# New written-out orders for kernel generation, two attention cores and two convolutions

## The chip, the cores and the metric

The kernel runs on one core of a Trainium2 chip. A core has five engines that run side by side, each from a queue of its own and each in the order of that queue: TensorE (PE in the profile; its weight loads are listed as PEld), VectorE (DVE), ScalarE (ACT), GpSimd (POOL) and SyncE (SP), which here issues DMA transfers. The metric is the device time of one execution in microseconds; lower is better. Times of several executions are given as their median.

## What is computed

The input x has 2048 rows of 512 values. Four layers follow one another, each adding its result to x: an attention, a long convolution, and both again with the same weights.

```python
x = x + _A_ref(_layernorm(x), A_wqkv, A_wo)
x = x + _B_ref(_layernorm(x), B_A_re, ..., B_Dskip)
x = x + _A_ref(_layernorm(x), A_wqkv, A_wo)
x = x + _B_ref(_layernorm(x), B_A_re, ..., B_Dskip)
```

The attention has 32 heads of 16 values. Each position looks at 8 positions: itself and those 2, 4, ... 14 before it. Logits, a softmax over the 8, a weighted sum of v, and a product with wo.

The convolution first makes, for each of the 512 channels, a kernel of 2048 values from a state of 128 complex numbers, then convolves each channel with it by Fourier transforms of length 4096, and adds u times Dskip:

```python
P = jnp.exp(logdA[:, :, None] * l[None, None, :])
K = jnp.einsum("dn,dnl,dn->dl", Cc, P, dB).real
...
y = irfft2(Uf * Kf)[..., :L] + u * Dskip
```

## The kernel before

**Stages.** The kernel goes through kernel generation together with the front of the first attention (0 to about 108 us), the first attention core (to about 191), the first convolution (to about 247), whose end overlaps the front of the second attention (about 243 to 273), the second core (to about 361) and the second convolution (to the end).

**What sets the order.** Inside each stage the instructions are emitted under `manual_schedule`: nothing reorders them, and each engine runs its queue as written. The order of a stage is a string. A function goes through its tokens and calls for each the small function that it stands for; that function puts its matmuls on PE's queue, its eviction on ACT's or DVE's, its transfers on SP's. So a string fixes the order of every queue at once. In the convolutions a token ends with the engine that evicts: `KD` is a step K evicted by DVE, `KA` by ACT.

**Kernel generation** (`ORDERK`, run by `k_gen`). The letters stand for the steps that build powers of the state (DVE products at L1115, ACT exponentials and sines), for the front of attention 1, and for the sums over the state on PE (L1273), whose results ACT evicts (L1281) and SP stores to `kd_dram` in 24 transfers (L1295). The front normalises the blocks `x_blk` (statistics, `ln_nb` at L1185, then an apply on DVE, L197, or ACT, L195; the table `ENGK` says which), transposes them on PE (L1201) and projects them (L1211).

**Attention core** (`CORE0`, `CORE1`, run by `LayerA.core`). The letters: `v` a projection of v (PE L398, ACT L400), `q` one of q (PE L223, ACT L225), `m` a product of q with the shifted k (DVE L342, 2.3 us), `l` its sum over the head (PE L350 or L354), `P` a product of the attention weights with the shifted v (DVE L472), `S` and `V` its sum (PE L487, L497), `O` the projection with wo (PE L508) with the statistics of the next norm, `a` to `f` and others steps of that norm. In `CORE0`, `1` and `6` load the two halves of the kernel from `kd_dram`, and `A` to `H` are its eight permuting copies `k_perm` (L1455), whose engines stand in `KROWS`. `w` loads `w_sb`, 4 MB of weights of the second transform stage (L596), into the place of q's and k's weights and of k, so it waits until the last product `m` has read them.

**Convolution** (`ORDER0` with the tail in `ORDERF`, then `ORDER1`, run by `FftB.run`). `K` and `U` are the first transform stage of the kernel and of the input (PE L807, eviction L796), `k` and `u` the second (PE L814; `k` evicted at L796, `u` always by ACT at L865), `m` the product of both spectra (DVE L852), `y` the first inverse stage (32 half matmuls, PE L883) and `Y` the same with 16 whole ones (PE L879), evicted at L796, `w` and `v` the second inverse stage, 8 or 4 blocks of rows for one group of columns (PE L927 to L929). `w` and `v` evicted by DVE add x on DVE (L931); evicted by ACT, x is added on PE by a further matmul and ACT copies (L933). In the first convolution every kernel spectrum is stored to `kf_dram` after its product and its buffer is used again by a later `k`; the second convolution loads them from there.

**Front of attention 2** (`ORDERF`, among the rest of the first convolution). `h`/`H`, `a`, `p` are statistics, `n` is the apply of a block (`D` DVE, `G` GpSimd and DVE in turns), `T` its transposes (PE L271), `E` a copy of half of them (L273), `P` and `Q` projections of k and q, `x` and `e` the copies that extend k.

Of the kernel before, what the change touches and what calls it, by code (L numbers as in the profile page):

```python
# [21 lines left out]
S = 2048  # L22
# [21 lines left out]
DQT = 8  # L44
NQT = DQG // DQT
ORDERK = """
isbCCisCbCiaisbMCiiMiMGGMsGCbicbMibMcsaTGMbiMsbicbTisTbGTMTTTiiGTaGbsaTibbciTGMTsibaMiMacGGTaalw
GMbMiaaMlWMMMalTsiyaMMyyyiMTMttaaMMdekaealTkMMbaMskMMalMKMaMqqkKiqMMWbQlMqqMHyyyUyaUUpQtxepakxkK
pqtUdUkpeUHUUQUkaUKUEqqUUkTQkU3TxTaqpqlKT3T3xalkQkKpkWTTxxTqlyq3kyyQppyqTKHTTxqQlWTUtktUekekklKx
KzkzkkkUUKUETUTzkkzttUUUUeKppUUUeKkkUEkxKkpoUkxpUxKXkUUKkxpUqxoUXpqxoQkppxKZXZxZ  # L50
"""
ORDER0 = """
KD KA KA KD KA KA KD KA KD KA KD kA KD KA KA KD UA UD UA kD kA UA kD UA UD UA
UA KD kD kA kD u m u u u kD UA m UA UA m u kD u m UD m kA UA kD UA
u m m UA UA kD kA u kD m u kA kA m u yD YD m u m u yA m u YA m
u u u m m m YA YA yA yD w000D YA yA
"""
LATE0 = "a s t g r b m"
ORDERF = """
yD yA yA yD yD YA w010A v101A v111A v110A h00 v100A h01 h11 w001A h10 a0 v112A S a1 p0 p1 n0D w011A  # L60
v102D T0 E01D n1G E00A v113D H2 v103A P02 a2 Q00 P01 p2 T1 E10D E11D P00 P03 n2G P11 P10 H3 P12 a3
T2 E20D p3 E21D n3D P13 P22 P23 T3 P20 E31D P21 E30D x1
"""
ORDER1 = """
UD UA UD UA UA UD UA UD UA UD UA u UD m u u u m u m UA u UA m m UA
UD u m m u u m u u yA m m yA yD m u u m u u YD m YA YA u w000A
yA yA m m m w001D yA yA w010D yA yA yA yA YD w011D YA v101D v102D v112D v111D v100A v110D v113A v103D
"""

CORE0 = """  # L70
vvvmvvlmqvqlxmevvlrmvlvnmlvmmTvqxllvqvvmqPemvqSrllPmqxn1OT0meVPrlP5S3POSqmOl2SPOSPOm4PlSlb7xn6O8
VOePSOdrAPSPPDnOSOSPCO9SbPOwHfPGVOfbPdFSBOEftSataaOfa
"""
CORE1 = """
0m1l2ml3mqqqlqmvvlmvvvmxqlemvvllrmvmnqlTqqmxvlmlevvvvqPvvvlmrPqlSnmmxOqSPTqeSPOPSlPOOmlSPrbSmnOP
SOwPllxdSOOVefPaaPaSrOnVPbOSOPSdPOPbVaOSdfOPatfaSfataO
"""
ROWS0 = (0, 2, 1, 3, 4, 5, 6, 7, 8, 9, 10, 11, 12, 13, 14, 15)
ROWS1 = (0, 2, 1, 3, 4, 5, 6, 7, 8, 9, 10, 11, 12, 13, 14, 15)
NCOL = (2, 2)  # L80
ENGK = dict(b="AAAAAAAAAAAAAAAAA", y="DAAAAAAAADAA", z="DAAA", e="AAAAAAAA", K="AAAAAAAAAAAAAAAA", Q="AAAAAAAA", x="AAAAAAAAAAAAAAAA")
STATD = (3,)
KROWS = "DADDDDDD"
VROWS = (*range(0, 16, 2), *range(1, 16, 2))


# [908 lines left out]
def k_gen(tc, nc, a_consts, ins, kd, la, x_v, lnst, zero, b_consts):  # L995
# [3 lines left out]
    with ExitStack() as ctx:  # L999
# [161 lines left out]
        def norms():  # L1161
            D2 = D * D
            for b in range(4):
                cs = slice(4 * b, 4 * b + 4)
                rstd = la.fp.tile([P, 4], F32, name="ln_rstd")
                nb = la.fp.tile([P, 4], F32, name="ln_nb")
                ln[b] = rstd, nb
                if b not in STATD:
                    mean, ms = lnst["s1"][:, cs], -1.0 / D
                    msq = la.fp.tile([P, 4], F32, name="ln_msq")  # L1170
                    veps = la.fp.tile([P, 4], F32, name="ln_veps")
                    lvar[b] = veps[:]
# [12 lines left out]
                yield lambda: nc.vector.scalar_tensor_tensor(nb[:], mean, ms, rstd[:], ALU.mult, ALU.mult)  # L1185
# [28 lines left out]
        def projected(kind, b, ft):  # L1214
            dst = la.kT[:, ft, 14 + b * 4:18 + b * 4, :] if kind == "k" else la.qT[b][:, ft]
            copy_by(ENGK["K" if kind == "k" else "Q"][4 * b + ft])(dst.rearrange("p a q -> p (a q)"), pps[kind, b, ft][:])  # L1216

# [59 lines left out]
        def produced(c, q8):  # L1277
            if (c, q8) == (0, 0):
                late["kgs"] = late["kgp"].tile([P, NB * 4, P], BF16, name="kgs")
            q0 = c * CH + q8 * 8  # L1280
            copy_by(ENGK["x"][c * CH // 8 + q8])(late["kgs"][:, :, q0:q0 + 8].rearrange("p m (h j) -> p m h j", h=2),  # L1281
                           pks[c, q8][:, :, 0:4 * NB * 4].rearrange("p h (j m) -> p m h j", j=4))
# [38 lines left out]
        def calls(f, *args):  # L1321
            return [lambda a=a: f(*a) for a in args]

        def chain(*fs):
# [59 lines left out]
def kernel(  # L1384
# [68 lines left out]
    def k_part(h, j):  # L1453
        cp = nc.scalar.copy if KROWS[h * 4 + j] == "A" else nc.vector.tensor_copy
        cp(kp[:, h * 64 + j * 16:h * 64 + (j + 1) * 16, :, :],  # L1455
           krs[h][:, :, j * 64:(j + 1) * 64].rearrange("p a (q r) -> p q a r", r=4))
# [128 lines left out]
```

## Time and profile before

| | us |
|---|---|
| median of three executions | 406.82 (406.75, 406.82, 409.1) |
| the profiled execution | 408.58 |
| its span, first to last instruction | 406.80 |

The profile is of one execution. "Busy" is the time in which an engine runs an instruction that does work. A row of a group has the busy time, the mean of one instruction, and after the second bar how long the engine stood idle just ahead of them and on whom it waited. A row of the timeline has the start, the duration, the engine, line and operation, and in brackets the idle time before it and what released it. `x4` in such a row means four like instructions in one row; their durations overlap a little at the ends, so the step from start to start is shorter than the duration of one. The granted TensorE clock over the span was 0.995 of full speed.

### The profile page before, as it was taken

How to read it: one execution, taken by the hardware profiler on the slowest of the kernel's cores; microseconds unless marked ns; L12 is line 12 of the kernel's file. 1: busy time of each engine (PE TensorE's matmuls, PEld its weight loads, DVE VectorE, ACT ScalarE, POOL GpSimd, SP SyncE). 2: the span in 40 equal slices, each digit the busy share in tenths (PEclk: the TensorE clock that was granted, in tenths of full speed). 3: DMA queues.
4: the chain of work that ended last, by engine and by line, in shares of the span. 5: the costliest groups of instructions: out<-in, count | busy, mean ns of one | idle time of the engine just before them, and what ended most of it. 6: DMA issues, size and time to landing. Idle time of an engine off the chain costs nothing.

```text
span 406.8 us, 14843 instructions
## 1 busy us (share of the span) xinstructions
PE 334.3 (82%) x6559; PEld 233.5 (57%) x6559; DVE 377.3 (93%) x454; ACT 324.6 (80%) x556; POOL 57.0 (14%) x77
## 2 busy tenths in 40 slices
PE   3000369999999999979998788999999999998795
PEld 2000117657635567656887788553455777667784
DVE  6999999999899999996999988989899999989975
ACT  7999978997555698867999896655566868889992
POOL 9302500000397000100500000300000020000000
PEclk9999999999999999989999999999999999999999
DMA  7942810423015755394046694550063037503616
GB/s 219 395 135 31 92 45 2 104 46 86 15 41 136 195 164 174 92 379 154 31 145 250 219 303 107 218 173 1 2 168 91 3 106 313 159 3 103 211 31 183
DMA packets 62322, 54.17 MB, mean 133 GB/s; under 512 B 33869, under 2 KB 50738, under 8 KB 60978
## 3 DMA queue, kind: packets, MB, share of 16 engines
q1 hardware_dynamic: 62250, 53.22, 43.0%
q8 instruction: 51, 0.84, 0.9%
q14 instruction: 13, 0.11, 0.1%
q10 hardware_dynamic: 8, 0.00, 0.0%
HBM read 30.15 MB, written 13.24 MB: 107 GB/s over the span
## 4 chain that ended last, share of the span: by engine, by line
PE 43%; DVE 29%; ACT 14%; issue 8%; DMA 4%; POOL 1%; SPq 0%; DVEq 0%; ACTq 0%; POOLq 0%
PE pq L398 7%; DVE pav L472 7%; PE pk L1273 6%; PE pq L223 4%; PE pp L1211 4%; DVE prod L342 3%; DVE B_t L1115 3%; PE pq L508 3%; PE pp L282 3%; ACT ub L865 3%; PE po L497 3%; DVE t L852 3%; DVE A_t L1115 2%; PE L L350 2%; PE pb L883 2%
## 5 line engine op out<-in xcount | busy, mean ns | idle before, releaser
L472 DVE TENSOR_TENSOR pav<-attn,v_ext 128x4096 bf16<-128x4096 bf16 (+1 forms) x34 | 72.4, 2157 | 2.6 <-PE po L487 1.6
L342 DVE TENSOR_TENSOR prod<-qT,kT_ext 128x4096 bf16<-128x4096 bf16 x29 | 66.3, 2315 | 3.7 <-PE L L350 1.7
L1115 DVE TENSOR_TENSOR A_t<-A_t,pow_t 128x1024 bf16<-128x1024 bf16 (+4 forms) x46 | 38.3, 872 | 0.3
L1201 PE MATMUL pt<-ident,x_blk 128*128 128x128 bf16 x64 | 5.7, 242 | 39.3 <-DVE x_blk L197 38.8
L508 PE MATMUL pq<-wop,oT 128*128 128x512 bf16 x128 | 33.2, 380 | 2.3 <-issue 2.1
L1211 PE MATMUL pp<-xnT,kT_ext 128*128 128x512 bf16 x96 | 28.5, 425 | 5.7 <-ACT kT_ext L1216 3.6
L497 PEld LDWEIGHTS <-pav 64*128 64x128 bf16 x1664 | 26.1, 95 | 9.8 <-DVE pav L472 3.9
L865 ACT CAST ub<-pb 128x1024 bf16<-128x1024 f32 x32 | 31.4, 1083 | 0.2 <-PE pb L814 0.2
L398 PE MATMUL pq<-wv,xnT 128*128 128x512 bf16 x128 | 30.7, 379 | 0.0
L497 PE MATMUL po<-ident,pav 64*128 64x64 bf16 x1664 | 29.0, 190 | 1.5 <-DVE pav L472 0.6
L796 ACT CAST a1s<-pb 128x1024 bf16<-128x1024 f32 x30 | 28.7, 1046 | 1.7 <-PE pb L807 1.6
L814 PE MATMUL pb<-a1s,w_sb 128*128 128x64 bf16 x768 | 27.3, 193 | 2.9 <-ACT a1s L796 1.0
L400 ACT CAST v_ext<-pq 128x512 bf16<-128x512 f32 x32 | 18.8, 586 | 13.0 <-PE pq L398 13.0
L1201 PEld LDWEIGHTS <-x_blk 128*128 128x128 bf16 x64 | 4.6, 108 | 41.0 <-DVE x_blk L197 39.1
L814 PEld LDWEIGHTS <-w_sb 128*128 128x128 bf16 x768 | 24.8, 98 | 5.1 <-issue 3.2
L1273 PEld LDWEIGHTS <-A_t 128*64 128x64 bf16 (+1 forms) x512 | 22.7, 107 | 4.5 <-DVE B_t L1115 0.8
L1273 PE MATMUL pk<-B_t,A_t 128*64 128x84 bf16 (+1 forms) x512 | 24.6, 206 | 0.0
L223 PE MATMUL pq<-xnT,kT_ext 128*128 128x512 bf16 x96 | 24.0, 380 | 0.0
L796 DVE CAST a1s<-pb 128x1024 bf16<-128x1024 f32 x18 | 21.5, 1217 | 2.4 <-PE pb L807 2.2
L225 ACT CAST qT<-pq 128x512 bf16<-128x512 f32 x24 | 14.1, 586 | 10.5 <-PE pq L223 10.5
L514 ACT ACTIVATE x_sb<-pq 128x512 bf16<-128x512 f32 x24 | 14.3, 595 | 8.8 <-PE pq L508 8.3
L398 PEld LDWEIGHTS <-xnT 128*128 128x128 bf16 x128 | 11.9, 98 | 14.4 <-issue 1.5
(249 smaller groups left out, 905.0 us busy)
## 6 DMA issues: line engine op xcount, KB each, us to landing
w_sb<-w_dram SPq DMA_DIRECT2D x8, 1024.0 KB, 6.7
w_dram<-xnT SPq DMA_DIRECT2D x1, 4096.0 KB
kf_ring<-kf_dram SPq DMA_DIRECT2D x13, 256.0 KB, 4.7
kf_ring<-kf_dram SPq DMA_DIRECT2D x26, 128.0 KB, 3.8
v_ext<-v_ext SPq DMA_DIRECT2D x4, 784.0 KB, 6.2
x_blk<-in_A_x_dram SPq DMA_DIRECT2D x4, 512.0 KB, 4.1
kT_ext<-in_A_wqkv_dram SPq DMA_DIRECT2D x4, 512.0 KB, 9.6
x_sb<-in_A_x_dram SPq DMA_DIRECT2D x4, 512.0 KB, 7.7
```

What stands on the lines that cost most here:

```text
L223: nc.tensor.matmul(pq[:], lhsT=self.wqk[:, dt, ft * P:(ft + 1) * P], rhs=self.xnT[:, dt, q * 512:(q + 1) * 512], start=(dt == 0), stop=(dt ...
L342: nc.vector.tensor_tensor(pr, self.qT[q][:, ft].unsqueeze(1).to_broadcast([P, W, 4, P]), kap, ALU.mult)
L398: nc.tensor.matmul(pp[:], lhsT=xnT[:, dt, a * P:(a + 1) * P], rhs=wv[:, dt, :], start=(dt == 0), stop=(dt == NDT - 1))
L472: nc.vector.tensor_tensor(pv[:, i], attn[:, n % 4].unsqueeze(2).to_broadcast([P, W, DH // parts, H]), vap, ALU.mult)
L497: nc.tensor.matmul(po[:, h, 0, i * nt + ft, :], lhsT=pvf[rows, i, w, ft * P:(ft + 1) * P], rhs=ident[rows, rows], start=(w == 0 and ft + i ...
L508: nc.tensor.matmul(pw[:], lhsT=oT[:, ftp, :], rhs=self.wo[:, ftp, :], start=False, stop=(ftp == NDT - 1))
L796: (self.nc.scalar.copy if eng == "act" else self.nc.vector.tensor_copy)(dst, src)
L814: nc.tensor.matmul(p2[:, j, :], lhsT=self.w2[:, ec * EC + j, :], rhs=a1s[:, ec * EC + j, :], start=True, stop=True)
L865: nc.scalar.copy(ub[:], p2)
L1115: return lambda: nc.vector.tensor_tensor(*args)
L1211: nc.tensor.matmul(pps[kind, b, ft][:], lhsT=la.wqk[:, dt, c:c + P], rhs=la.xnT[:, dt, b * 512:(b + 1) * 512], start=(dt == 0), stop=(dt = ...
L1273: nc.tensor.matmul(o, lhsT=lhs, rhs=Bt[:, ri, c * CH + ql].rearrange("p b g -> p (b g)"), start=(not half and j % 4 == 0 and ri == 0), sto ...
```

## The change

Only strings and tables change; no function does. All six orders are written anew, `ENGK["y"]`, the engines of twelve applies in the first front, has one `D` at the eleventh place where it had two, at the first and the tenth, and `KROWS` gives two copies (`D` and `E`) to ACT where it gave one (`B`).

```diff
 ORDERK = """
-isbCCisCbCiaisbMCiiMiMGGMsGCbicbMibMcsaTGMbiMsbicbTisTbGTMTTTiiGTaGbsaTibbciTGMTsibaMiMacGGTaalw
-GMbMiaaMlWMMMalTsiyaMMyyyiMTMttaaMMdekaealTkMMbaMskMMalMKMaMqqkKiqMMWbQlMqqMHyyyUyaUUpQtxepakxkK
...
+sCGiCiCCbsbiisCiiCGMMbiMGsMibMabisMbibMGbaaMTcsMGcbcGiTTGTisTTiTabiMGcTTbbsibTaiaTTbMsTGMGciiGMa
+aMaMlaaibMsMlwMaWaiMlaMyyyTMMiaytbMMetMMeadklMkKsaMlMWMMkqMakiqMKqQMaqQlbqMMkHqyTUypkUypUKxakpUU
...
 ORDER0 = """
-KD KA KA KD KA KA KD KA KD KA KD kA KD KA KA KD UA UD UA kD kA UA kD UA UD UA
-UA KD kD kA kD u m u u u kD UA m UA UA m u kD u m UD m kA UA kD UA
-u m m UA UA kD kA u kD m u kA kA m u yD YD m u m u yA m u YA m
-u u u m m m YA YA yA yD w000D YA yA
+KD KA KA KA KD KA KD KA KD KA KD kA KD KA kA kD UA KD UA KD UA UA kD UA UD UA
+UD KA kA kD u kD u m u kD UA UA UA UA m m kD u kD m u UA kA u m u
+UD kD m UA UA u m kD u kA m kA kA u m yD u m yA YD m u u u m m
+YA u u yA m YA m yA m YA w000D YA
 ...
 ORDERF = """
-yD yA yA yD yD YA w010A v101A v111A v110A h00 v100A h01 h11 w001A h10 a0 v112A S a1 p0 p1 n0D w011A
-v102D T0 E01D n1G E00A v113D H2 v103A P02 a2 Q00 P01 p2 T1 E10D E11D P00 P03 n2G P11 P10 H3 P12 a3
-T2 E20D p3 E21D n3D P13 P22 P23 T3 P20 E31D P21 E30D x1
+YD yA yD yA yA yA YD w010A v101D h01 v111A h11 v110A h00 v100A h10 w001A a0 a1 p0 p1 z12A v103A S
+n0D n1G w011A T0 E00D E01A H2 v113A a2 P03 T1 E11A P00 E10D H3 P02 a3 P12 p2 Q00 P13 P10 n2D P11
+T2 E20D p3 E21A P01 P20 P21 n3D T3 E30D x1 E31D P23 P22
 ORDER1 = """
-UD UA UD UA UA UD UA UD UA UD UA u UD m u u u m u m UA u UA m m UA
-UD u m m u u m u u yA m m yA yD m u u m u u YD m YA YA u w000A
-yA yA m m m w001D yA yA w010D yA yA yA yA YD w011D YA v101D v102D v112D v111D v100A v110D v113A v103D
+UA UD UA UD UA UA UD UA UD UA UD u UD u UA m u m u m u UD m UA u m
+UA u m u m u u m u m m u yD YA yA m YA m u u YD m YA u u YA
+YA m m m w001A w000D yA yA w011D YA w010D yA yD yA yD yA v100D v101A v111D v110D v103D v113A v112D v102D
 CORE0 = """
-vvvmvvlmqvqlxmevvlrmvlvnmlvmmTvqxllvqvvmqPemvqSrllPmqxn1OT0meVPrlP5S3POSqmOl2SPOSPOm4PlSlb7xn6O8
-VOePSOdrAPSPPDnOSOSPCO9SbPOwHfPGVOfbPdFSBOEftSataaOfa
+vvmvvvmlxvqlevmqlrmvnvmlTqlvmmqvlvvvxmPlevvmrl1nqlSTPm0xqmVPeOrl5PqSP2OmlSOS3ql4POSOP78mSPnlOxP6
+DbVeOSPrOSPnPOSOPSOSPd9bOVAfPOCEawSafPbOdtaSfOatBGfFH
 CORE1 = """
-0m1l2ml3mqqqlqmvvlmvvvmxqlemvvllrmvmnqlTqqmxvlmlevvvvqPvvvlmrPqlSnmmxOqSPTqeSPOPSlPOOmlSPrbSmnOP
-SOwPllxdSOOVefPaaPaSrOnVPbOSOPSdPOPbVaOSdfOPatfaSfataO
+0m1l2ml3mqqvmvvllvmvqmvqxllevqmrlmvnmlvTqqqxlvmmPqvvlPvmvvvlqelSrqmnOSxmTqPSPeOSlrOPPlSmOSOPSlnm
+PPOlSOxVeOPPSbrOnVbPdaPOSafOPVaPdOSbawPaOdfSOfaaStftfO
 ...
-ENGK = dict(b="AAAAAAAAAAAAAAAAA", y="DAAAAAAAADAA", z="DAAA", ...)
+ENGK = dict(b="AAAAAAAAAAAAAAAAA", y="AAAAAAAAAADA", z="DAAA", ...)
-KROWS = "DADDDDDD"
+KROWS = "DDDAADDD"
```

One token in the new orders has no counterpart in the old ones: `z12A` in `ORDERF` does the second inverse stage of four blocks for both column groups of a half at once (eviction of 128x4x256 by ACT, L914), in place of two `v`.

More of the change, by code (lines that the diff above doesn't have):

```diff
@@ L46 @@
 ORDERK = """
-isbCCisCbCiaisbMCiiMiMGGMsGCbicbMibMcsaTGMbiMsbicbTisTbGTMTTTiiGTaGbsaTibbciTGMTsibaMiMacGGTaalw
-GMbMiaaMlWMMMalTsiyaMMyyyiMTMttaaMMdekaealTkMMbaMskMMalMKMaMqqkKiqMMWbQlMqqMHyyyUyaUUpQtxepakxkK
-pqtUdUkpeUHUUQUkaUKUEqqUUkTQkU3TxTaqpqlKT3T3xalkQkKpkWTTxxTqlyq3kyyQppyqTKHTTxqQlWTUtktUekekklKx
-KzkzkkkUUKUETUTzkkzttUUUUeKppUUUeKkkUEkxKkpoUkxpUxKXkUUKkxpUqxoUXpqxoQkppxKZXZxZ
+sCGiCiCCbsbiisCiiCGMMbiMGsMibMabisMbibMGbaaMTcsMGcbcGiTTGTisTTiTabiMGcTTbbsibTaiaTTbMsTGMGciiGMa
+aMaMlaaibMsMlwMaWaiMlaMyyyTMMiaytbMMetMMeadklMkKsaMlMWMMkqMakiqMKqQMaqQlbqMMkHqyTUypkUypUKxakpUU
+xpQUyxHUkUattqqUeKUUqQEeTakxqkTUQkKTUUaqkdTa3lqKp3lp3WxlyxypkTypTyTkQtT3tTlHxqqTWKeQTUklUTzkeUkT
+KTUkzUUUKkkzkUzUkKtKtpUUeUxkkEUxKkepxkKkkoKpxkEUUqkUoUpUqxpKUxUXpxpkkQxKpoZXZXZx
 """
 ORDER0 = """
-KD KA KA KD KA KA KD KA KD KA KD kA KD KA KA KD UA UD UA kD kA UA kD UA UD UA
-UA KD kD kA kD u m u u u kD UA m UA UA m u kD u m UD m kA UA kD UA
-u m m UA UA kD kA u kD m u kA kA m u yD YD m u m u yA m u YA m
-u u u m m m YA YA yA yD w000D YA yA
+KD KA KA KA KD KA KD KA KD KA KD kA KD KA kA kD UA KD UA KD UA UA kD UA UD UA
+UD KA kA kD u kD u m u kD UA UA UA UA m m kD u kD m u UA kA u m u
+UD kD m UA UA u m kD u kA m kA kA u m yD u m yA YD m u u u m m
+YA u u yA m YA m yA m YA w000D YA
 """
@@ L80 @@
 NCOL = (2, 2)
-ENGK = dict(b="AAAAAAAAAAAAAAAAA", y="DAAAAAAAADAA", z="DAAA", e="AAAAAAAA", K="AAAAAAAAAAAAAAAA", Q="AAAAAAAA", x="AAAAAAAAAAAAAAAA")
+ENGK = dict(b="AAAAAAAAAAAAAAAAA", y="AAAAAAAAAADA", z="DAAA", e="AAAAAAAA", K="AAAAAAAAAAAAAAAA", Q="AAAAAAAA", x="AAAAAAAAAAAAAAAA")
 STATD = (3,)
-KROWS = "DADDDDDD"
+KROWS = "DDDAADDD"
 VROWS = (*range(0, 16, 2), *range(1, 16, 2))
```

## The prediction

> **What bounds the kernel now.** I read the page's summary, then busy time by stage, then single waits.
>
> ```profile
> span 406.8 us, 14843 instructions
> PE 334.3 (82%) x6559; PEld 233.5 (57%) x6559; DVE 377.3 (93%) x454; ACT 324.6 (80%) x556; POOL 57.0 (14%) x77
> PE 43%; DVE 29%; ACT 14%; issue 8%; DMA 4%; POOL 1%; SPq 0%; DVEq 0%; ACTq 0%; POOLq 0%
> L472 DVE TENSOR_TENSOR pav<-attn,v_ext 128x4096 bf16<-128x4096 bf16 (+1 forms) x34 | 72.4, 2157 | 2.6 <-PE po L487 1.6
> L342 DVE TENSOR_TENSOR prod<-qT,kT_ext 128x4096 bf16<-128x4096 bf16 x29 | 66.3, 2315 | 3.7 <-PE L L350 1.7
> ```
>
> VectorE (DVE) is busy 93% of the span, and its two big groups, the attention products, are not touched by the change in number or form. Yet the chain that ended last runs 43% on TensorE (PE) and 29% on DVE, so no engine carries the whole. The busy times by stage say who is full where; the columns are PE, weight load, DVE, ScalarE (ACT), GpSimd, granted clock, DMA share, GB/s.
>
> ```profile
> 40.00:61.00 21.00, 9.28 (x32) 3.86 (x33) 20.97 (x33) 17.98 (x40) 6.42 (x3) 1.00 0.52 69
> 61.00:108.00 47.00, 45.72 (x645) 32.34 (x647) 46.41 (x69) 40.09 (x75) 0.00 (x0) 1.00 0.22 52
> 108.00:136.00 28.00, 28.00 (x242) 12.33 (x235) 25.59 (x14) 16.78 (x27) 21.57 (x16) 1.00 0.38 96
> 136.00:191.00 55.00, 50.95 (x1253) 35.68 (x1252) 51.83 (x47) 44.50 (x94) 1.05 (x1) 0.97 0.59 185
> 191.00:243.00 52.00, 45.91 (x1378) 41.52 (x1378) 48.69 (x50) 49.61 (x56) 6.41 (x9) 1.00 0.56 200
> 243.00:273.00 30.00, 28.44 (x378) 20.38 (x371) 25.75 (x70) 19.03 (x35) 3.52 (x4) 1.00 0.54 173
> 273.00:361.00 88.00, 86.70 (x1541) 51.03 (x1538) 84.62 (x72) 62.19 (x130) 2.92 (x1) 1.00 0.30 97
> 361.00:393.00 32.00, 27.25 (x848) 25.28 (x850) 29.95 (x27) 30.80 (x34) 0.00 (x0) 1.00 0.34 102
> 393.00:406.80 13.80, 8.89 (x248) 8.54 (x244) 7.38 (x9) 6.49 (x8) 0.00 (x0) 0.98 0.52 154
> ```
>
> Kernel generation (to 108) is DVE's: 46.41 of 47 in its second half. The second attention core (273 to 361) is PE's, 86.70 of 88. The convolutions (191 to 243, 361 to 393) belong to ACT and DVE together. So a DVE instruction moved to ACT pays in kernel generation and in the first core, and pays nothing in the second core or the convolutions.
>
> **The change, part by part.** All six order strings are new. In the queues as built, DVE has four instructions fewer, ACT five more, GpSimd two fewer, PE some fifty fewer (three more inverse transforms use the whole form, of 16 matmuls for 32); "nine" and "eleven" come out when equal neighbours on a queue are folded into one row.
>
> *Kernel generation.*
>
> ```profile
> 44.58 1.21 DVE L1115 TENSOR_TENSOR A_t<-A_t,A_t 128x2048 bf16<-128x2048 bf16 x1
> 45.71 0.68 DVE L1090 TENSOR_TENSOR sq_z<-ws 128x512 f32<-128x512 f32 x1
> 57.31 0.42 DVE L1115 TENSOR_TENSOR B_t<-B_t,cm_t 128x512 bf16<-128x512 bf16 x1
> 46.77 0.50 PE L1201 MATMUL pt<-ident,x_blk 128*128 128x128 bf16 x3 [38.83 <-DVE x_blk L197]
> 55.99 2.29 PE L1211 MATMUL pp<-xnT,kT_ext 128*128 128x512 bf16 x5 [2.81 <-ACT kT_ext L1216]
> L197 DVE TENSOR_SCALAR x_blk<-x_blk,ln_rstd,ln_nb 128x512 bf16<-128x512 bf16 x3 | 1.2, 404 | 0.0
> L195 ACT ACTIVATE x_blk<-x_blk,ln_nb,ln_rstd 128x512 bf16<-128x512 bf16 x13 | 9.9, 815 | 0.1
> ```
>
> One normalisation of x_blk leaves DVE for ACT: DVE saves 0.40, ACT pays 0.815 of its idle 3.0 in 40 to 61. DVE's work ahead of the level that follows is otherwise the same, so -0.40. Against it, three more DVE instructions stand ahead of the first ln_nb (L1185): one each of the first three rows, 1.21 + 0.68 + 0.42 = 2.3 (some 2.1 net of overlap). PE's transposes, which began at 46.77, begin that much later, and the fourth apply on ACT may add 0.8: 2.9 in all. PE had only 9.28 of 21 to do there and waited 2.81 on ACT's evictions at 55.99, so I count it at nothing; uncovered, it costs up to 2.9.
>
> *First core.*
>
> ```profile
> 108.73 15.62 SPq L1295 DMA_DIRECT2D kd_dram<-kgs  x24
> 132.64 2.29 DVE L472 TENSOR_TENSOR pav<-attn,v_ext 128x4096 bf16<-128x4096 bf16 x1 [0.67 <-DMA v_ext<-v_ext]
> 172.28 2.24 SPq L596 DMA_DIRECT2D w_sb<-w_dram  x4
> 176.00:178.70 2.70, 2.70 (x72) 1.49 (x71) 2.67 (x6) 2.36 (x7) 0.00 (x0) 1.00 1.01 422
> 178.70:180.90 2.20, 0.06 (x2) 0.03 (x1) 2.20 (x3) 0.28 (x2) 0.00 (x0) 1.00 1.02 425
> 180.90:184.30 3.40, 3.40 (x31) 3.16 (x31) 1.42 (x4) 2.12 (x5) 0.00 (x0) 0.51 0.96 405
> 184.70 2.36 DVE L472 TENSOR_TENSOR pav<-attn,v_ext 128x2048 bf16<-128x2048 bf16 x2 [1.61 <-PE po L487]
> L1455 DVE COPY k_perm<-k_rl 128x1024 bf16<-128x1024 bf16 x7 | 2.8, 415 | 0.0
> L1455 ACT COPY k_perm<-k_rl 128x1024 bf16<-128x1024 bf16 x1 | 1.0, 1047 | 0.0
> ```
>
> At 132.64 DVE waits 0.67 for a copy of v that SyncE issues behind 24 stores of the kernel. The last level of kernel generation stands earlier in the new order, so its stores start earlier and I take this wait as gone: -0.67 (bounds 0 and -0.67). At 184.70 DVE waits 1.61 for the sum L487 of product 13: PE stood still from 178.7 to 180.9 and then ran at a granted clock of 0.51, while the 4 MB load of w_sb held the DMA engines at 0.96 to 1.02. The new order puts one k_perm copy and two short statistics steps between products 14 and 15, about 1.0 of DVE work that stood after the wait: -1.0. One k_perm copy goes to ACT, whose own is 1.05 there: -0.42 on DVE. Together -1.4. From below: 0, if the wait merely grows; from above the 3.8 that PE loses there, 2.14 (2.20 - 0.06) and 3.40 x 0.49 = 1.67. I take the small value because PE reaches the same place with the load still under way.
>
> [...]
>
> *First convolution.*
>
> ```profile
> 220.51 2.35 DVE L852 TENSOR_TENSOR t<-ub,kf_nat 128x2048 bf16<-128x2048 bf16 x2
> 222.56 0.59 SPq L855 DMA_DIRECT2D kf_dram<-kf_nat  x1
> 227.26 1.93 ACT L796 CAST kf_nat<-pb 128x1024 bf16<-128x1024 f32 x2 [1.47 <-DMA kf_dram<-kf_nat]
> ```
>
> K, k, U, u and m keep their number. The one place where the ring of kernel tiles is short is at 227.26: ACT waits 1.47 to evict k14 until the tile that product m5 read (220.51) is stored (issued 222.56, landed about 227.2, so 4.7). In the new order m5 and m6 stand one DVE step later, 2.35 - 1.22 = 1.13, and k14 stands where it stood on ACT. ACT has 2.4 of 52 idle there, so I count +1.1; bounds 0 (DVE is as late as ACT) and +7.9 (below).
>
> *Front of the second attention layer.*
>
> ```profile
> 256.28 0.69 DVE L273 COPY xnT<-pt 128x1024 bf16<-128x1024 bf16 x1 [0.40 <-PE pt L271]
> 269.84 1.29 DVE L273 COPY xnT<-pt 128x1024 bf16<-128x1024 bf16 x2 [0.99 <-PE pt L271]
> L931 DVE TENSOR_TENSOR x_sb<-pb,x_sb 128x512 bf16<-128x512 f32 x8 | 5.2, 684 | 0.7 <-PE pb L929 0.7
> L273 DVE COPY xnT<-pt 128x1024 bf16<-128x1024 bf16 x7 | 4.5, 675 | 1.4 <-PE pt L271 1.4
> L197 DVE TENSOR_SCALAR xn<-x_sb,ln_rstd,ln_nb 128x512 bf16<-128x512 bf16 x12 | 4.6, 440 | 0.2
> ```
>
> DVE loses one residual add (0.68) and two transpose copies (2 x 0.675) and takes two applies from GpSimd (2 x 0.44): -1.15. But blocks 2 and 3 now have the apply, the transposes and the copy one behind the other on DVE, PE and DVE; block 3 had that already, at 0.99. Two such waits for the 0.40 + 0.99 of now: +0.59. Sum -0.56, between -1.15 and +2 (each wait behind eight matmuls under way on PE).
>
> *Second core.* One apply goes from DVE to ACT (0.4 by the rows above), in a stage with PE busy 86.70 of 88: counted 0. Two more projections stand ahead of one lsum:
>
> ```profile
> L398 PE MATMUL pq<-wv,xnT 128*128 128x512 bf16 x128 | 30.7, 379 | 0.0
> 391.54 5.79 ACT L796 CAST z<-pb 128x1024 bf16<-128x1024 f32 x6
> ```
>
> Eight matmuls at 30.7/128 = 0.24 are 1.9 that the product behind the lsum may wait; its cover is the products already queued on DVE. Bounds -1 and +1.9.
>
> *Second convolution.* DVE has the same 25 steps up to m15. ACT now evicts first, so DVE starts about half an ACT step later: +0.5. After m15, ACT has six evictions of y in place of seven, each 5.79/6 = 0.97, in a tail where PE is busy only 8.89 of 13.8: -0.97. Sum -0.5, bounds -2 and +1.5.
>
> Sum: -0.40 - 0.67 - 1.4 + 1.1 - 0.56 + 0 - 0.5 = -2.4. The profiled execution took 408.58 (span 406.80 and 1.78 around it) and is 1.76 above the median 406.82, so 408.58 - 2.4 = 406.2 there, and **404.4** as a median.
>
> **The rivals.**
> (a) *Faster: the standstill of PE goes.* If PE is past its place before the DMA share reaches 1, all 3.8 come back, of which 1.4 is counted: 404.4 - 2.4 = 402.0, and 400 if the starts behind it close up. For it: PE stops nowhere else for "issue" so long. Against: the load is released by the last product of that stage, which moves with PE.
> (b) *Slower: the same standstill grows.* If the load saturates the DMA engines 2 earlier relative to PE, PE stops 2.0 longer and stays at the half clock for another 1.7, and the 1.4 is not won: 404.4 + 1.4 + 3.7 = 409.5. It decides once PE reaches its place less than about 0.5 after the share reaches 1.0; now that is 2.7 (176.0 to 178.7). [...] By the trace 2.2 of idleness was enough at 178.7, and 2.81 ahead of 55.99 was not (1.00 in 40 to 61), so length alone does not decide, and I use the row.
> (c) *Slower: the ring of the first convolution.* If the stores of m5 and m6 are issued one after the other behind the half swaps that SyncE has queued, k14 and k15 each wait a whole 4.7: 9.4 for 1.47, +7.9 in place of +1.1: 404.4 + 6.8 = 411.2. It decides when those stores are issued only after ACT has arrived at k14. For it: the new order has fewer steps between m5 and k14. Against: k15 waited nothing of its own at 227.26.
> (d) *PE's late start in kernel generation isn't absorbed:* 404.4 + 2.9 = 407.3. PE is full from 61 on; but DVE is too.
>
> **How the numbers follow.** Forecast 0.37, own range 400.5 to 408.5; (a) 0.22; (b) 0.16; (c) 0.17; (d) 0.08. One per cent, about what a measurement of this kernel can tell from no change, is 4.07: faster is below 402.75, slower above 410.89. Faster: 0.13 of the forecast's 0.37 (a third of its range lies below 402.75) and 0.19 of (a): 0.32. Slower: 0.08 of (b), half of it by the spread around 409.5, 0.11 of (c), and 0.05 of the forecast's and (d)'s upper ends: 0.24. The rest, 0.44, is within. The range goes from 399, the lower end of (a), to 412.5, past (c).
>
> **What would show it.** Right: the wait on v_ext at the first pav gone; DVE's wait at the last pav of the first core under 1.0; a wait of ACT on kf_dram of about 2.6; two waits of about 1.0 on pt L271 in the front; the last y evicted by ACT about 1 earlier after m15. A gap of PE with "issue" and a stretch at half clock near 177 to 184 must be there; without them (a) holds, longer by 2 or more (b). A wait on kf_dram above 5 in sum is (c); less PE time in 61 to 108 and a later end of it is (d). I am wrong altogether if the time moves by more than 2 in a stage for which I have written 0.

## The result and the profile after

The changed kernel takes 404.08 us as a median of twenty executions (400.43 to 408.44), the kernel before 407.93 (twenty, 405.43 to 409.71). The ratio is 0.9904 with a 95% interval of 0.9884 to 0.9925: about 1% faster. The prediction had 404.4, as 2.4 less than a median of 406.82 of three executions; the measured medians differ by 3.9.

The profiled execution of the changed kernel took 400.43, the lowest of the twenty, and its span is 8.1 shorter than that of before, twice what the medians differ by. A second profile of each kernel was therefore needed (e1 and e2 below). First the page of the first one: span, busy time, the chain that ended last.

```profile
span 398.7 us, 14678 instructions
PE 324.2 (81%) x6456; PEld 231.7 (58%) x6503; DVE 373.8 (94%) x450; ACT 327.7 (82%) x561; POOL 62.9 (16%) x75
PE 49%; DVE 28%; issue 10%; ACT 8%; DMA 2%; SPq 2%; POOL 1%; DVEq 0%; ACTq 0%; POOLq 0%
```

DVE has 3.5 us less to do and ACT 3.1 more. That is about the size of the moved work; the time did not follow it stage by stage. The next table has stage lengths, worked out from the starts of the same instructions in the timelines: the first pav (L472), the first eviction of K on DVE (L796), the sixteenth product of the convolution (L852), the first copy of turned rows in the front (L273, second layer), the first product of the second convolution.

| stage, us | before | before again (e1) | changed | changed again (e2) |
|---|---|---|---|---|
| start to first pav | 132.64 | 134.20 | 130.77 | 131.66 |
| to first K | 59.57 | 59.43 | 56.05 | 56.67 |
| to last product of conv. 1 | 45.70 | 45.65 | 45.43 | 47.34 |
| to first copy of the front | 18.37 | 17.74 | 18.04 | 21.58 |
| to first product of conv. 2 | 112.74 | 112.85 | 111.38 | 111.37 |
| to the end | 37.77 | 37.64 | 36.99 | 36.99 |
| span | 406.79 | 407.51 | 398.66 | 405.61 |

The last two stages repeat within 0.13 between the two profiles of a kernel. The others differ by up to 1.6 (the first, before) and, in the changed kernel, by 1.9 in the third and 3.5 in the fourth. The busy times of the first core, in the changed kernel and then in the kernel before again, by windows cut at those starts (columns as above: PE, weight load, DVE, ACT, POOL, clock, DMA share, GB/s):

```profile
130.80:186.80 56.00, 52.19 (x1280) 36.11 (x1295) 54.70 (x48) 47.91 (x100) 3.01 (x1) 1.00 0.63 201
269.70:361.70 92.00, 89.62 (x1761) 57.03 (x1776) 88.00 (x75) 68.06 (x135) 1.02 (x1) 1.00 0.29 94
```

```profile
134.20:193.60 59.40, 51.69 (x1271) 36.70 (x1284) 55.19 (x48) 47.26 (x97) 1.05 (x1) 0.97 0.58 186
276.70:369.90 93.20, 89.86 (x1759) 57.05 (x1775) 88.77 (x76) 67.07 (x134) 2.92 (x1) 1.00 0.29 92
```

In the first core DVE is busy nearly as long in both, but idle 1.3 instead of 4.2, and the clock is 1.00 instead of 0.97. In the second core DVE's busy time falls by 0.77 and the stage by 1.2.

The rows that the prediction named, from the changed kernel's timeline and its list of waits:

```profile
130.77 2.28 DVE L472 TENSOR_TENSOR pav<-attn,v_ext 128x4096 bf16<-128x4096 bf16 x1
177.60 1.95 PE L487 MATMUL po<-ident,pav 128*128 128x128 bf16 x32 [1.25 <-ACT x_sb L514]
179.81 2.35 DVE L472 TENSOR_TENSOR pav<-attn,v_ext 128x2048 bf16<-128x2048 bf16 x2
239.03 1.23 DVE L796 CAST z<-pb 128x1024 bf16<-128x1024 f32 x1 [1.15 <-PE pb L879]
259.55 0.69 DVE L273 COPY xnT<-pt 128x1024 bf16<-128x1024 bf16 x1 [1.23 <-PE pt L271]
263.06 0.69 DVE L273 COPY xnT<-pt 128x1024 bf16<-128x1024 bf16 x1 [1.26 <-PE pt L271]
```

```profile
ACT kf_sb L796 <- DMA kf_dram<-kf_sb: 1.1, 1, 1.1
ACT kf_nat L796 <- DMA kf_dram<-kf_nat: 0.2, 1, 0.2
```

In this profile the first and the last pav wait for nothing (before: 0.67 and 1.61; e2: 0.78 and 0.29). The two new waits of the front are there, 1.23 and 1.26. ACT's wait on the ring is 1.1 + 0.2 and is met one tile earlier. Under the load of w_sb PE waits 1.25, and the profile names ACT as what ended the wait. The run e4 below shows that this is the standstill of the kernel before again, shorter and without a stretch at half clock behind it.

### The profile page after: what moved, and what is told of

It is laid out like the page before. It is cut to its first block, busy times and chain, and to the rows that moved or that the text cites. A ratio compares the mean times of both kernels' runs of the same rounds, so it can differ in the third digit from the quotient of the medians.

```text
span 398.7 us, 14678 instructions
## 1 busy us (share of the span) xinstructions
PE 324.2 (81%) x6456; PEld 231.7 (58%) x6503; DVE 373.8 (94%) x450; ACT 327.7 (82%) x561; POOL 62.9 (16%) x75
## 4 chain that ended last, share of the span: by engine, by line
PE 49%; DVE 28%; issue 10%; ACT 8%; DMA 2%; SPq 2%; POOL 1%; DVEq 0%; ACTq 0%; POOLq 0%
PE pq L398 7%; PE pk L1273 5%; PE pq L508 5%; DVE pav L472 4%; PE po L497 4%; PE pq L223 4%; DVE prod L342 3%; DVE B_t L1115 3%; PE pp L282 3%; DVE A_t L1115 3%; PE pp L1211 3%; DVE a1s L796 3%; DVE t L852 2%; PE pb L807 2%; ACT ub L865 2%
## 5 line engine op out<-in xcount | busy, mean ns | idle before, releaser
L472 DVE TENSOR_TENSOR pav<-attn,v_ext 128x4096 bf16<-128x4096 bf16 (+1 forms) x34 | 72.1, 2156 | 0.0
L1201 PE MATMUL pt<-ident,x_blk 128*128 128x128 bf16 x64 | 5.8, 241 | 42.2 <-ACT x_blk L195 42.2
L1115 DVE TENSOR_TENSOR A_t<-A_t,pow_t 128x1024 bf16<-128x1024 bf16 (+4 forms) x46 | 37.7, 869 | 0.2
L508 PE MATMUL pq<-wop,oT 128*128 128x512 bf16 x121 | 31.3, 379 | 2.5 <-issue 2.1
L497 PEld LDWEIGHTS <-pav 64*128 64x128 bf16 x1664 | 25.9, 95 | 9.4 <-issue 6.1
L1201 PEld LDWEIGHTS <-x_blk 128*128 128x128 bf16 x64 | 4.6, 108 | 43.9 <-ACT x_blk L195 43.2
L796 ACT CAST a1s<-pb 128x1024 bf16<-128x1024 f32 x30 | 29.0, 1066 | 0.9 <-PE pb L807 0.8
L497 PE MATMUL po<-ident,pav 64*128 64x64 bf16 x1664 | 28.8, 190 | 0.2 <-ACT oT L499 0.2
L1211 PE MATMUL pp<-xnT,kT_ext 128*128 128x512 bf16 x88 | 24.4, 393 | 4.9 <-ACT kT_ext L1216 2.4
L1273 PEld LDWEIGHTS <-A_t 128*64 128x64 bf16 (+1 forms) x512 | 21.7, 103 | 4.3 <-DVE A_t L1115 0.5
L1273 PE MATMUL pk<-B_t,A_t 128*64 128x84 bf16 (+1 forms) x512 | 23.5, 201 | 0.4 <-DVE A_t L1115 0.4
L223 PE MATMUL pq<-xnT,kT_ext 128*128 128x512 bf16 x89 | 23.0, 379 | 0.5 <-issue 0.2
L178 POOL TENSOR_TENSOR ln_rstd<-ln_rstd,ln_mh 128x4 f32<-128x4 f32 x2 | 4.0, 2014 | 119.6 <-DVE ln_msq L170 83.6
L796 DVE CAST a1s<-pb 128x1024 bf16<-128x1024 f32 x18 | 21.2, 1214 | 1.8 <-PE pb L807 1.7
L508 PEld LDWEIGHTS <-oT 128*128 128x128 bf16 x128 | 12.5, 98 | 12.4
```

The costliest lines, as they stand in the source:

```text
L223: nc.tensor.matmul(pq[:], lhsT=self.wqk[:, dt, ft * P:(ft + 1) * P], rhs=self.xnT[:, dt, q * 512:(q + 1) * 512], start=(dt == 0), stop=(dt ...
L472: nc.vector.tensor_tensor(pv[:, i], attn[:, n % 4].unsqueeze(2).to_broadcast([P, W, DH // parts, H]), vap, ALU.mult)
L497: nc.tensor.matmul(po[:, h, 0, i * nt + ft, :], lhsT=pvf[rows, i, w, ft * P:(ft + 1) * P], rhs=ident[rows, rows], start=(w == 0 and ft + i ...
L508: nc.tensor.matmul(pw[:], lhsT=oT[:, ftp, :], rhs=self.wo[:, ftp, :], start=False, stop=(ftp == NDT - 1))
L796: (self.nc.scalar.copy if eng == "act" else self.nc.vector.tensor_copy)(dst, src)
L1115: return lambda: nc.vector.tensor_tensor(*args)
```

## The experiments

Ratios are to the kernel before, run on the same chip.

### Both kernels again (e1, e2)

No edit.

> The kernel before, unchanged, for a second profile. If PE's standstill near 178.7 (2.1 us idle for no releaser, then half clock) hangs on the place of the 4 MB load against PE's work, it comes again within 1 us of the same matmul, and the span to the last pav (184.70) repeats within 1 us. If it is an accident of that execution, PE runs through, and the last pav starts 2 to 4 us earlier. Time: 1.000 of the kernel before within 0.3%.

> The changed kernel, unchanged, for a second profile beside the one of 400.43 us, which was the lowest of its twenty executions (median 404.08). If the standstill comes and goes by execution, this profile is longer by 2 to 5 us and shows PE idle for no releaser somewhere under the load of w_sb (168 to 179). If the new order escapes it, the last pav starts at 179.8 again within 1 us. Ratio 0.990 within 0.003.

Ratios 0.9996 (0.9966 to 1.0027) and 0.9932 (0.9907 to 0.9957). From the timelines of the kernel before again:

```profile
134.20 2.29 DVE L472 TENSOR_TENSOR pav<-attn,v_ext 128x4096 bf16<-128x4096 bf16 x1 [2.63 <-DMA v_ext<-v_ext]
182.37 0.58 PE L508 MATMUL pq<-wop,oT 128*128 128x512 bf16 x1 [2.08 <-issue]
186.13 2.36 DVE L472 TENSOR_TENSOR pav<-attn,v_ext 128x2048 bf16<-128x2048 bf16 x2 [1.50 <-PE po L487]
```

and of the changed kernel again, with three of its windows:

```profile
179.11 1.95 PE L487 MATMUL po<-ident,pav 128*128 128x128 bf16 x32 [1.72 <-ACT ln_junk L145]
242.22 0.20 PE L883 MATMUL pb<-Wp,t 64*128 64x64 bf16 x2 [1.86 <-issue]
245.83 1.23 DVE L796 CAST z<-pb 128x1024 bf16<-128x1024 f32 x1 [4.52 <-PE pb L879]
```

```profile
225.00:229.00 4.00, 3.71 (x73) 3.56 (x73) 2.06 (x3) 3.66 (x4) 0.00 (x0) 0.57 0.57 204
240.40:242.20 1.80, 0.00 (x0) 0.00 (x0) 0.91 (x1) 0.16 (x1) 0.00 (x0) 1.00 0.01 1
242.20:246.00 3.80, 3.78 (x88) 3.69 (x88) 0.17 (x1) 2.84 (x3) 0.00 (x0) 0.55 0.02 4
```

The standstill of the kernel before came again at the same matmul (2.08 after 2.14), so it is no accident of one execution. At the same place the changed kernel has 1.72 here after 1.25, again put down to ACT. It also has a standstill of its own in this execution, at the end of the first convolution: PE does nothing for 1.8, then 3.8 at a clock of 0.55, and DVE waits 4.52 for one block where it waited 1.15 in the first profile. That stage is 3.5 longer, half of the 7 us between the two profiles of the changed kernel.

Another 1.9 come earlier, up to the last product: ACT waits 1.82 on kf_dram where it waited 1.11, and behind that the clock is at half for 3.4 us from 225.49 (0.57 in the window above; 1.00 at the same place of the first profile). The wait for v_ext differs as well between executions of one kernel, 0.67 and 2.63.

### The load of w_sb in quarters (e3, e4)

```diff
-        for c in range(4):
+        for c in range(1 if part else 4):
             self.nc.sync.dma_start(self.w2[:, c * 32:(c + 1) * 32, :], ...)
+    def load_w2_more(self, w2_dram, c):
+        self.nc.scalar.dma_start(self.w2[:, c * 32:(c + 1) * 32, :], ...)
 CORE0
-...PGVOfbPdFSBOEftSataaOfa
+...PGXVOfbPdYFSBOEfZtSataaOfa
```

X, Y and Z call `load_w2_more` for the quarters 1, 2 and 3.

> The kernel before, with the second, third and fourth quarter of the w_sb load issued from ScalarE's queue later in the first core (about 184, 187 and 190) in place of all four at 172 from SyncE. If PE starves because the load fills the DMA engines, the idle time without a releaser near 178.7 and the half clock are gone, the last pav starts 2 to 3 us earlier, and the time falls by 1.5 to 3 us (ratio 0.993 to 0.996). If the standstill has nothing to do with the load, it stays at the same matmul and the time is equal or up to 1 us longer (three issues on ScalarE).

> The same edit in the changed kernel. If most executions of the changed kernel still lose time to the load, the median falls by 1 to 3 us against the changed kernel; if the new order already escapes it, the time is that of the changed kernel within 1 us (ratio 0.988 to 0.993).

Ratios 0.9973 (0.9951 to 0.9995) and 0.9918 (0.9886 to 0.9951). PE's waits in e3 (in total, how many, the longest), then the same place in e4, from its timeline and its windows:

```profile
PE pq L508 <- issue: 3.5, 15, 1.3
```

```profile
176.24 1.95 PE L487 MATMUL po<-ident,pav 128*128 128x128 bf16 x32
176.57 0.58 ACT L514 ACTIVATE x_sb<-pq 128x512 bf16<-128x512 f32 x1
172.00:173.20 1.20, 1.04 (x65) 1.03 (x61) 1.20 (x1) 1.17 (x3) 0.00 (x0) 1.00 0.12 41
173.20:176.20 3.00, 2.84 (x72) 1.74 (x73) 2.95 (x6) 2.55 (x8) 0.00 (x0) 1.00 0.00 0
```

In e3 the standstill is at the same matmul but 1.3 long, and no half clock follows. One quarter, issued at 173.01, is enough to keep the DMA engines at a share of 0.94 from 174.8 to 177.8. In e4 that quarter is issued at 167.05, the engines are nearly idle from 172.0 on, and the matmul L487 that waited 1.25 and 1.72 in the changed kernel starts without a wait. It also starts ahead of ACT's L514, which the profile had named in the first of those two. So it is not ACT that this matmul waits for; the wait comes and goes with the load.

Neither version gains much in total, and the stages show why. The first core of e3 takes 56.35 where the kernel before took 59.5, and its next stage 1.0 more (46.69). The first core of e4 takes 54.89, and its next stage 48.90, with a half clock from 225.96.

### The parts alone (e5 to e8)

```diff
 e5: ORDERK, ENGK of the changed kernel
 e6: CORE0, KROWS of the changed kernel
 e7: ORDER0, ORDERF of the changed kernel
 e8: CORE1, ORDER1 of the changed kernel
```

> The kernel before with the new order of kernel generation and its table alone. Stages add up: in two profiles of the changed kernel the first product after that stage starts 1.1 us earlier (111.15 to 110.03) and the first pav 1.0 to 1.9 earlier, so 0.7 to 1.9 us less at K0 and a ratio of 0.995 to 0.999. If the gain only moves a wait, the first pav is earlier and K0 is not, and the ratio is 1.000.

> The new order of the first core and the engines of its k_perm copies alone. Stages add up: from the first pav to K0 the changed kernel needs 2.9 to 3.5 us less in its two profiles (56.05 and 56.67 for 59.57), of which 1.4 was forecast; ratio 0.991 to 0.994. If most of that was the standstill of PE and not the order, it is 1.4 or less: 0.996 to 0.999, with the idle time without a releaser at an equal matmul count.

> The new orders of the first convolution and of the front of the second attention alone. From K0 to the first product of the second attention but one (m17) the changed kernel took 82.8 us in one profile and 88.3 in another, the kernel before 83.8 and 83.1. If the new order is worth -0.6 plus 1.1 as forecast, the ratio is 1.001; if it loses to PE's standstill at 240 in most executions, 1.004 to 1.010; if it gains as in the first profile, 0.997.

> The new orders of the second core and the second convolution alone. From m17 to the end the changed kernel took 129.0 us in both its profiles, the kernel before 130.8 in both, so -1.8 us: ratio 0.995 to 0.997. The forecast had -0.5 there (0.999).

| | ratio | interval |
|---|---|---|
| e5, kernel generation | 0.9938 | 0.9915 to 0.9961 |
| e6, first core | 0.9998 | 0.9968 to 1.0028 |
| e7, first convolution and front | 1.0053 | 1.0025 to 1.0082 |
| e8, second core and convolution | 0.9988 | 0.9963 to 1.0014 |

e7 came out in the range set for a standstill near 240 (1.004 to 1.010), but its profile has just 0.77 there; it also has a half clock from 221.83. e5 gained more than expected, e6 and e8 less (e8 is where the forecast had it, 0.999). The four sum to -0.23%, the whole change is -0.96%. The four intervals together allow some 0.5% either way, so the parts fail to add up by little more than the noise. PE's waits show one reason. They are, in this order, of e5, of e6 and of e8:

```profile
PE pq L508 <- issue: 2.4, 15, 0.2
PE po L487 <- ACT x_sb L514: 1.4, 1, 1.4
```

```profile
PE pq L508 <- issue: 4.2, 15, 2.0
PE pb L927 <- issue: 2.0, 1, 2.0
PE po L497 <- issue: 1.0, 1, 1.0
PE pb L883 <- issue: 1.0, 1, 1.0
```

```profile
PE pq L508 <- issue: 4.2, 14, 2.2
```

With the new kernel generation alone the wait at L508 is gone, though the core's order is the old one. It has moved to the next matmul of the queue, L487, is 1.4 long, and is put down to ACT again; no half clock follows it. With the new core alone it stays at L508, and three more of 1 to 2 us appear. In e8 it is there with its full 2.2, but this time the clock stays up behind it:

```profile
178.80:181.10 2.30, 0.13 (x2) 0.06 (x1) 2.30 (x3) 0.32 (x3) 0.00 (x0) 1.00 0.98 406
181.10:184.50 3.40, 3.40 (x58) 2.50 (x59) 2.61 (x6) 2.77 (x7) 0.00 (x0) 1.00 1.02 426
```

### The old first convolution in the changed kernel (e9)

```diff
 e9: the changed kernel with ORDER0, ORDERF of the kernel before
```

> The changed kernel with the old orders of the first convolution and of the front of the second attention. If the parts add up, the loss of 0.5% that these two orders alone gave goes, and the ratio is 0.985 to 0.988 (about 402 us). If the new orders fit only each other, it is 0.990 or above.

Ratio 0.9919 (0.9889 to 0.9948). The 0.5% that these orders cost in e7 they do not cost here: the ratio is that of the changed kernel, in the range set for orders that fit only each other. In the one profile the third stage is shorter (44.93), but the first core takes 57.56 and the last stage 38.05, 1.2 and 1.1 more than in the profiles of the changed kernel. So a loss measured in one context did not carry over to another.

### Moving the blocks of instructions (e10, e11)

```diff
             pt = xps[b, d] = la.ps_tr.tile([P, 2, 4, P], BF16, name="pt")
+            if len(xps) == 1:
+                for i in range(64):
+                    nc.tensor.transpose(pt[:, i // 4 % 2, i % 4, :], ident[:], ident[:])
```

> The kernel before with 128 more instructions on TensorE (64 transposes of the identity ahead of the first real transpose, in time that TensorE waits anyway). In all profiles so far TensorE's long waits without a releaser stand at a count of its matmuls and weight loads that is 148 to 193 over a multiple of 256. If they come from the fetching of instructions in blocks of 256, they now stand 128 instructions earlier or later in the program, at the same counts modulo 256, and none is at the fourth matmul of the output projection after product 13. If the standstill belongs to that projection, it stays there, at a count modulo 256 that is 128 more (40 to 65). Time: 0.993 if TensorE happens to wait at the new place, 1.000 if not.

> The same 128 instructions in the changed kernel, where two of three profiles had a wait of 1.4 to 1.9 us near 240 at the count 7078 and lost 2 to 5 us behind it. If blocks set the place, no wait is at that program step, and any wait without a releaser over 0.4 us stands at a count of 148 to 193 modulo 256; the time then tells whether the new places cost less (ratio 0.982 to 0.987) or more (0.992 to 0.998). If the place belongs to the program step, the wait is there again and the ratio stays at 0.990.

Ratios 1.0045 (1.0014 to 1.0077) and 1.0038 (1.0009 to 1.0068), above every value that was expected. The profiled execution of e10 took 415.48, the longest of its twelve (median 410.37). One row of its timeline and one of its waits, then one row of the timeline of e11:

```profile
245.83 0.21 PE L883 MATMUL pb<-WpJ,t 64*128 64x64 bf16 x1 [3.99 <-issue]
```

```profile
PE po L497 <- issue: 2.4, 3, 1.2
```

```profile
242.56 0.24 PE L883 MATMUL pb<-Wp,t 64*128 64x64 bf16 x2 [2.79 <-issue]
```

A count here is that of all TensorE records of a trace: matmuls, weight loads and the few semaphore and drain instructions. No wait over 0.2 is left at the output projection L508 in e10; the ones that came instead stand at L497 (counts 3265, 4033, 4289) and at L883 (7361). In e11 they are at 2753, 4033, 4289, 7361 and 12993. Every one of these counts is 193 over a multiple of 256, as are 2497, 4033 and 7105 in the first profile of before. (Where some records are missing from a trace, the remainder falls along it, from 179 to 146, in steps.) The place is set by the count of instructions, not by the program step. The 1.25 and 1.72 of the changed kernel at L487 stand at 4033 too, the count of the 2.14 of before: a wait at the end of a block can be put down to an engine that had nothing to do with it.

The trace also records the transfers of instructions, on a queue of their own. The row of the page of before (transfers, MB, share of the DMA engines):

```profile
q8 instruction: 51, 0.84, 0.9%
```

TensorE has 13142 records in that trace (6559 matmuls, 6559 weight loads, 24 semaphore and drain instructions), so one transfer for every 258. Their starts, beside the time at which PE passed the count where a block ends:

| profile | PE passes a block's end | next transfer starts | after | PE comes to the next block's end | PE waits | goes on, after the transfer's start |
|---|---|---|---|---|---|---|
| before, count 3265 | 163.4 | 164.1 | 0.7 | 169.6 | 0 | |
| before, 3777 | 174.5 | 178.4 | 3.9 | 178.7 | 2.14 | 2.45 |
| e3, 3752 | 174.8 | 177.8 | 3.0 | 179.0 | 1.31 | 2.5 |
| changed, 3752 | 172.0 | 175.3 | 3.3 | 176.4 | 1.25 | 2.35 |
| e2, 3752 | 173.0 | 176.7 | 3.7 | 177.4 | 1.72 | 2.4 |
| e4, 3752 | 172.0 | 173.2 | 1.2 | 176.2 | 0 | |
| changed, 6824 | 233.3 | 234.2 | 0.9 | 236.8 | 0 | |
| e2, 6824 | 236.8 | 239.7 | 2.9 | 240.4 | 1.86 | 2.55 |

(3752 is the place 3777 in a trace that lacks 25 records by then; 6824 is 6849.) Between the first two times of a row the share of the DMA engines is 0.28 and 0.82 in the rows with 0.7 and 0.9, 0.12 in e4, and 0.94 to 1.04 in the other five. So where the engines were that full the next transfer started 2.9 to 3.9 after the end of a block. In those five rows PE came to the next block's end 0.3 to 1.2 after the transfer's start and stood still for 1.25 to 2.14; in the three rows where it came 2.6 to 5.5 after it, it did not wait. The fourteen traces have 33 waits of over 0.5 in which a matmul stands at such a count, and each ends 2.2 to 2.9 after the start of a transfer.

### Fewer instructions in the dense stretch (e12)

```diff
 ORDERF
-YD yA yD yA yA yA YD w010A ...
+YD YA YD YA YA YA YD w010A ...
```

> The changed kernel with the five half inverse steps (y) at the start of the front's order made whole (Y): 5 x 32 matmuls and as many weight loads less. In the changed kernel's profile five y in a row ran 160 matmuls and 160 weight loads in 2.3 us, so 256 instructions last 1.9 us there; whole steps ran 16 matmuls in 0.89 us, so 256 instructions last 7. If TensorE starves because it eats a block of 256 faster than the next one comes, no wait without a releaser over 0.4 us is left between 230 and 246 and the clock stays at 1.00 there, at a price of 5 x 0.42 = 2.1 us of matmul time; the ratio is 0.985 to 0.990 if what was lost is more than that, 0.990 to 0.994 if not. If the rate of instructions isn't the cause, the wait is there in spite of it and the ratio is 0.994 or more.

Ratio 0.9978 (0.9945 to 1.0011). Two windows at the place where e2 stood still, then a row of the timeline near the end:

```profile
240.40:242.20 1.80, 1.80 (x37) 1.80 (x33) 0.04 (x1) 1.80 (x3) 0.00 (x0) 1.00 0.00 0
242.20:246.00 3.80, 3.80 (x72) 3.80 (x70) 2.65 (x5) 2.44 (x4) 0.00 (x0) 1.00 0.54 153
```

```profile
395.71 0.22 PE L928 MATMUL pb<-z,g_sb 128*128 128x128 bf16 x1 [1.17 <-issue]
```

PE is full there and the clock 1.00: the standstill is gone, as expected if the rate of instructions causes it. It is one profile, and the first profile of the changed kernel has no standstill there either, so the table above carries the argument. The stretch from the last product to the front's first copy is 20.2 (254.06 - 233.89), 1.4 less than in e2 and 2.1 more than in the first profile, which is the price of five whole steps. A whole step has 16 matmuls and 16 weight loads less than a half one, so the edit takes away 160 instructions, half of what the expectation counted, and moves every later block's end. The end at 12737 now falls on a matmul L928, and PE waits 1.17 there; in both profiles of the changed kernel it falls on one of L883 and PE does not wait. The ratio came out above both ranges expected with the wait gone, 0.5% to 0.7% over the changed kernel. As a cure this edit does not pay.

No version was clearly faster than the changed kernel.

## Why the prediction was right

The median was forecast within 0.3 us, but the terms of the sum were not: errors in both directions cancelled. The starting point was off as well, 406.82 from three executions where twenty give 407.93, so a change of -2.4 was forecast and -3.9 measured. Point by point, with the stage table (means of both profiles of each kernel) and the single parts:

*Kernel generation and the wait on v_ext.* Forecast -0.40 - 0.67. Measured -2.2 up to the first pav, and 0.6% alone. The mechanism of the two terms was right, their size was not: the fourth product of q and k starts 1.1 and 0.7 earlier than in the two profiles of before (110.03 for 111.15 and 110.74), and the rest is the wait on v_ext, which in the seven profiles with the old order was 0.17 to 2.63 (mean 1.14) and in the seven with the new one 0 to 0.78 (mean 0.22). I had read it from one execution, where it was 0.67. PE's late start was absorbed, as counted: the first transposes begin 1.0 later and the last state sum on PE (L1273) ends 1.5 to 1.9 earlier. Rival (d) is out.

*First core.* Forecast -1.4, measured -3.1 in the whole change and 0 alone (e6, 59.61 in this stage). The step that failed is the pair of terms -1.0 and -0.42, for DVE work taken out from behind the wait: e6 has that same order, and its last pav still waits 1.90. What the runs show in its place is the half clock.

- Where a half clock follows the standstill at count 4033 (before, e1, e6, e7), DVE waits 1.47 to 1.90 at the last pav and the stage takes 59.4 to 59.6, in the old order and in the new.
- Where none follows it, DVE waits 0 to 0.59 and the stage takes 54.9 to 58.7. In e8, with the old order and a standstill of 2.17, it is 0.15 and 57.95. Only e10 is as long without it (59.32), with other standstills and a half clock from 162.03.

"PE reaches the same place with the load still under way" was right, and PE did stand still there. So rival (a) did not happen: the standstill became shorter by 0.4 to 0.9 and lost its half clock, which was worth 1.7, together some 2.0 to 2.6 of the 3.1 by estimate. The shortening goes with the order of kernel generation, not with that of the core. With the new kernel generation the wait stands at L487 and is 1.25 to 1.82 long in five profiles (changed, e2, e5, e9, e12), also in e5 with the old core; with the old one it stands at L508 and is 1.99 to 2.17 in five (before, e1, e6, e7, e8), also in e6 with the new core. Two semaphore instructions less stand ahead of it in the new one, so the same count falls on the next matmul. What the order of the core is worth by itself was not separated from this. Of the signs named, the gap of PE is there and the half clock is not. Rival (b) did not happen.

One reading behind rival (b) was wrong. These two rows of the kernel before have four like matmuls each:

```profile
59.38 1.86 PE L1211 MATMUL pp<-xnT,kT_ext 128*128 128x512 bf16 x4 [0.67 <-ACT kT_ext L1216]
66.84 1.04 PE L1211 MATMUL pp<-xnT,kT_ext 128*128 128x512 bf16 x4
```

From start to start one takes 0.427 in the first row and 0.216 in the second. The transposes (L1201) from 46.77 to 48.78 have 0.106, those from 64.97 on 0.056. The trace's record of the clock begins only at 64.89, and the windows give 1.00 for 40 to 61 all the same. In the changed kernel the record begins at 54.60, and the steps at L1211 fall from 0.43 to 0.22 between 54.47 and 55.14. So by the steps the clock was still at half from 46.77 to 61, and the wait of 2.81 ahead of 55.99 says nothing about how long a gap the clock bears.

*First convolution.* Forecast +1.1 by the ring. ACT waited 1.35 and 2.06 on kf_dram in the two profiles where 2.6 was forecast, against 1.47 before, so the ring added 0.6 at most by itself and (c) is out. Yet a loss of that size is there in most executions, by another way. Without e3 and e4, whose load of w_sb runs later, the stage takes 44.93 to 45.71 in the seven profiles with the old order (mean 45.4) and 45.42 to 47.34 in the five with the new one (mean 46.6). In four of these five, and in e4, the clock is at half for 3.4 us somewhere between 215 and 230; in none of the eight with the old order is it. In e2, e4 and e12 PE's waits behind the ring stand just ahead of it; in e7 and e11 PE waits 1.9 and 2.1 for other evictions, whose cause was not traced. The 3.5 that e2 loses behind the last product are PE's standstill, its half clock, and the waits behind them. I had counted the three whole steps and the five y in a row as nothing, and did not ask how fast they use up instructions.

*Front.* Forecast -0.56 with two waits of 1.0; the waits are 1.23 and 1.26, and from the first copy to the second product of that layer the stage gained 0.35.

*Second core.* Forecast 0, because PE is full. Measured -1.1 from that product to the first one of the second convolution (93.1 to 92.0), and e8 has the same alone (92.1). The step "pays nothing in the second core" was wrong: DVE, busy 88.8 of 93.2, is about as full as PE (89.9), and its 0.77 less came through. That this is the whole of it was not tried.

*Second convolution.* Forecast -0.5, measured -0.7 in these profiles. It does not hold throughout: the same order takes 38.46 in e8 and 38.05 in e9, where before has 37.7.

Added up by stage, -2.2, -3.1, +0.7, +1.8, -1.4 and -0.7 make -5.0 for these four profiles, 407.15 to 402.13; the medians, over many executions, differ by 3.9.

## What to carry to other kernels

Read the count modulo 256 of every long TensorE wait, also of those for which the profile names a releaser. Here it was 193, where no record was missing, at the waits that ended 2.2 to 2.9 after the start of an instruction transfer, and 128 instructions more, far ahead in the program, moved the places (e10, e11). To test a named releaser, look for a run in which the same instruction starts before it. Bursts of small matmuls under a big transfer are where such waits stood here; spreading the load or thinning the burst shortened or removed them there (2.14 to 1.31 in e3, 1.25 to 0 in e4, 1.86 of e2 to 0 in e12), but gained 0.3% at most (e3). Judge a reorder by its parts with care: here they gave -0.23% for -0.96%. Where one profile and the median disagree by 4 us, take another profile before explaining a stage.

## What the hardware showed that was not expected

TensorE stood still for up to 3.99 us (e10) for want of instructions, as the counts and the transfers have it, at the ends of blocks of 256; in the five such rows of the table the DMA engines were at a share of 0.94 to 1.04 until the transfer started. Whether a half clock follows depends on more than the length: after 2.08 to 2.14 of standing still it came in both profiles of before (0.51 and 0.52 for 3.4 us), after 2.17 in e8 it did not (1.00). Within one execution the traces have the changes of the clock a whole number of windows of 3.413 apart: in the first profile of before its record begins at 64.89 and changes at 180.94, 184.35 and 406.22, 34, 1 and 65 windows on; the stretches at half clock start in e10 at 162.03 and 243.95, 24 of them apart, in e2 at 225.49 and 242.55, five. That the wait counts by the part that falls into one window is my reading of such numbers. The 2.14 of before lie wholly between 177.53 and 180.94; the 2.17 of e8 are cut at 179.27, counted back from its record at 404.55, into 0.41 and 1.76. Over the fourteen traces every recorded window with TensorE idle for more than 2.0 was followed by half clock; between 1.5 and 2.0 some were (in the changed kernel the one from 392.52, with 1.97 idle, not the one from 245.75, with 1.72). Two stretches do not fit: in e5 from 159.74 and in e10 from 162.03, behind windows with 0.3 and 1.2 of idleness.

And 128 instructions more, early and in time in which TensorE was idle, made both kernels slower, by 0.45% and by 1.3% (1.0038 for 0.9904), as far as the profiles show by moving the blocks' ends into denser stretches: the waits at count 7361 are 3.99 and 2.79, with 6.8 and 3.4 us of half clock around them.
